# The uncast first w1 piece of an attention and soft-MoE kernel, loaded in three transfers of 32, 32 and 64 partitions instead of one of 128

## The chip, the cores and the metric

The kernel runs on one core of a Trainium2 chip. The metric is the device time of one execution in microseconds. Five executions of the kernel before took 178.75 to 179.28 us, with a median of 178.91 us.

## What is computed

The reference has two stages. The first is attention in 8 batches of 8 heads, 576 tokens and a head size of 64. Heads 0 to 3 see the last 32 tokens, heads 4 to 7 see every fourth of the last 128. The second stage takes the attention output as 4608 rows of 512 and sends it through a soft mixture of 8 experts with 4 slots each:

```python
scores = np.where(masks, scale * (q @ k.T), -1e9)          # per batch and head
x = (softmax(scores) @ v)                                   # -> 4608 x 512
logits = x @ phi                                            # 4608 x 32 slots
slot_input = softmax(logits, over tokens).T @ x             # 32 x 512
for e in range(8):
    h = np.maximum(slot_input[e] @ w1[e], 0.0)              # w1[e]: 512 x 1024
    slot_out[e] = h @ w2[e]                                 # w2[e]: 1024 x 512
out = softmax(logits, over slots) @ slot_out                # 4608 x 512, float32
```

All inputs and the output are float32. The two expert matrices come to 2 MB each per expert, q, k and v to 9.4 MB each, the output to 9.4 MB.

## The kernel before

The kernel is one program of scheduled operations. Each is declared with `op(engine, function, duration, priority, reads, writes)`. A planner (`Sched.run`) simulates the engines and one DMA queue with the estimated durations. It picks the order of the operations on each engine, and `emit` then writes them out with semaphore waits taken from the declared reads and writes.

**Loads.** q, k and v come in 16 half-batches (4 heads each, L334) of three transfers, and the weights in 35 further pieces (w1 by L344, w2 by L352 and L359). All of them are issued by GpSimd (POOL), because they are cast from float32 to bf16 on the way. Their order is fixed in `dma_order`: k, q, v of a half-batch, then one or no weight piece, and the rest of the weights after the last half-batch. The staging buffers of q, k and v hold four half-batches, so a later load waits until VectorE has transposed what stands in its buffer (L477, L483).

**The one load that is not cast.** The first half of expert 0's w1 (rows 0 to 255, 1 MB) is issued by SyncE (SP) at L387, as the first instruction of its queue. It lands as float32 in the space that w2 of expert 4 takes much later (`w2off(4)`). Partition p gets rows 2p and 2p+1, which are 8 KB in one run. ScalarE (ACT) then casts it to bf16 in two halves (L392, 1024 columns each) into w1's place. ACT's first other work is the exponential of the first scores (L537). SP's next instruction is the load of phi (L454), after that come only the output stores (L911).

**Compute.** Each half-batch goes through transposes on VectorE (L477), scores on TensorE (L498 to L522), the exponential on ACT (L537), the transpose of v (L559, L565), the product with v (L592 to L616), normalisation on VectorE (L599, L603), and, after each second half-batch, the logits and the slot sums (L682 to L736). When all are done, the experts run: L808 to L832 for w1, L847 for w2. The w2 products start as their pieces arrive. The output tiles (L890, evicted by L899 and L902) are stored by SP. Columns 0 to 255 of three row groups can go before the last w2 pieces are there.

The transfer in question and its readers:

```python
op(SP, lambda: spq.dma_start(af(w2off(4), [[1, 2048]]), moe_w1[0, 0:256, :].rearrange(...)),
   ..., sem=sem("s_w1f"), writes=b_w2[4], name="w1f")
for x in range(2):
    op(ACT, ..., reads=b_w2[4], writes=[b_w1[0]], name=f"w1c{x}")
```

Of the kernel before, what the change touches and what calls it, by code (L numbers as in the profile page):

```python
# [54 lines left out]
class Sched:  # L55
# [8 lines left out]
    def op(self, eng, fn, dur, prio, reads=(), writes=(), rmw=(), after=(), banks=(), name="",  # L64
           kind="c", nbytes=0, rate=422e3, lag=0.0, sem=None, tail=False):
        o = Op()
        o.eng, o.fn, o.dur, o.prio, o.name = eng, fn, dur, prio, name
        o.kind, o.bytes, o.rate, o.lag, o.sem, o.tail = kind, nbytes, rate, lag, sem, tail
        o.deps, o.succ = set(), []
        o.banks, o.opens, o.ord = [], [], None  # L70
        o.seq = len(self.ops)
        for a in after:
            if a is not None:
                o.deps.add(a)
        for b in reads:
            o.deps.update(b.w)
            b.r.append(o)
        for b in writes:
            if b.r:
                b.prev = b.w + b.r  # L80
                b.w, b.r = [], []
            o.deps.update(b.prev)
            b.w.append(o)
        for b in rmw:
            o.deps.update(b.prev)
            o.deps.update(b.w)
            o.deps.update(b.r)
            b.w.append(o)
        for b in list(reads) + list(writes) + list(rmw) + list(banks):
            if isinstance(b, Bank) and b not in o.banks:  # L90
                o.banks.append(b)
                if b.left == 0:
                    o.opens.append(b)
                b.left += 1
        o.deps.discard(o)
        self.ops.append(o)
        return o
# [99 lines left out]
def bass_dilated_sliding_attn__then__soft_moe_slots_kernel(  # L197
# [65 lines left out]
    def af(off, dims, p0=0, pn=128):  # L263
        return AP(ar_f.tensor, (p0 * NBF + off) // 2, [[NBF // 2, pn]] + dims)
# [12 lines left out]
    op = sc.op  # L277
    PE, ACT, DVE, POOL, SP = "PE", "ACT", "DVE", "POOL", "SP"
    pe, act, dve, pool, spq = nc.tensor, nc.scalar, nc.vector, nc.gpsimd, nc.sync
# [26 lines left out]
    b_w2 = [[Buf(f"w2{e}{s}") for s in range(2)] for e in range(8)]  # L306
# [6 lines left out]
    def w2off(e):  # L313
        return o_w2 + e * 8 * DM if e < 5 else o_stg + (e - 5) * 8 * DM


    def sem(n):
        return [nc.alloc_semaphore(n), 0]
# [54 lines left out]
    def load_w(n):  # L373
# [10 lines left out]
                   lag=(2.9 if name[2] == "s" else 2.3) if name[:2] == "w2" else 0.8, prio= -100.0 if nw[0] < 2 else -80.0, name=name, writes=list(wr) + rd)  # L384


    op(SP, lambda: spq.dma_start(  # L387
        af(w2off(4), [[1, 2048]]),
        moe_w1[0, 0:256, :].rearrange("(p two) f -> p (two f)", two=2)), .1, -200.0,
       kind="dma", nbytes=1 << 20, sem=sem("s_w1f"), writes=b_w2[4], name="w1f")  # L390
    for x in range(2):
        op(ACT, lambda x=x: act.activation(  # L392
            a(o_w1 + 1024 * x, [[1, 1024]]), af(w2off(4) + 2048 * x, [[1, 1024]]), ACTF.Copy),
# [379 lines left out]
    for x, y in zip(dma_order, dma_order[1:]):  # L773
# [7 lines left out]
       writes=[b_rcol], name="cs")  # L781
# [19 lines left out]
    for x in range(2):  # L801
# [12 lines left out]
        for g in range(2):  # L814
# [5 lines left out]
            writes=[b_hsb[x], b_p[0], b_p[1]], name=f"RL{x}")  # L820
# [39 lines left out]
    for y in range(2):  # L860
# [3 lines left out]
       name="SOx")  # L864
# [139 lines left out]
```

## Time and profile before

| | |
|---|---|
| five executions | 178.75 to 179.28 us, median 178.91 us |
| the profiled execution | 179.28 us, of which the span from first to last instruction is 177.5 us |
| busy share: TensorE, VectorE, ScalarE, GpSimd | 72%, 66%, 59%, 28% |
| mean granted TensorE clock | 0.938 |
| DMA | 41.29 MB written, mean 233 GB/s; HBM read and written 402 GB/s |
| queue of the GpSimd loads (q0) | 30.41 MB, 90.8% of 16 engines' span |
| queue of the SyncE transfers (q1) | 10.55 MB, 15.7% |
| the transfer of L387 | 1024 KB, issued at 0.74 us, landed after 5.0 us |

The profile counts DMA by what is written. A GpSimd load writes bf16 and reads twice as much, so 212 GB/s of such loads are 424 GB/s of reading. The DMA share is the time that packets took, divided by the time of 16 DMA engines. It can pass 1 because packets of one DMA engine overlap a little. The q0 and q1 queues are served by the same 16 DMA engines.

### The profile page before, as it was taken

Reading aid. Unit: us, or ns where it says so; the run is one execution under the profiler, and the core shown is the slowest. Engines: PE = TensorE matmul, PEld = TensorE weight load, DVE = VectorE, ACT = ScalarE, POOL = GpSimd, SP = SyncE. Lnnn points to the kernel's source line nnn. Section 1 sums busy time; section 2 is a strip of 40 time slices with the busy share of each in tenths; the row PEclk is TensorE's granted clock in tenths of the full one; section 3 lists DMA queues with packets and bytes.
Section 4 is the critical chain, followed back from the end, with each engine's and each line's share of the span. In section 5 each row is a group of like instructions: output and inputs, shape, how many; then the busy total and the mean of one; then the engine's idle time right before and its main releaser. Section 6 shows DMA issues by size and latency. Waiting matters only on the chain.

```text
span 177.5 us, 5201 instructions
## 1 busy us (share of the span) xinstructions
PE 127.8 (72%) x2173; PEld 86.6 (49%) x2174; DVE 117.7 (66%) x224; ACT 105.2 (59%) x166; POOL 50.3 (28%) x100
## 2 busy tenths in 40 slices
PE   0019768885999989889879988996596658698000
PEld 0006556664767677567567667684443223341000
DVE  6889578798899999798588999653300013499300
ACT  2406298886889799779748979794202012299000
POOL 7469931423413432332770000392000000000000
PEclk9999999999999999999978999999969987999655
DMA  5999999999999999999999999999999999999997
GB/s 188 229 211 215 214 207 212 216 206 212 217 210 208 217 207 211 217 209 210 215 207 212 213 210 217 213 212 214 213 215 210 203 196 178 285 321 398 417 423 314
DMA packets 19606, 41.29 MB, mean 233 GB/s; under 512 B 1920, under 2 KB 9088, under 8 KB 18688
## 3 DMA queue, kind: packets, MB, share of 16 engines
q0 software_dynamic: 15024, 30.41, 90.8%
q1 hardware_dynamic: 4560, 10.55, 15.7%
q8 instruction: 17, 0.28, 0.6%
q14 instruction: 5, 0.04, 0.1%
HBM read 61.93 MB, written 9.44 MB: 402 GB/s over the span
## 4 chain that ended last, share of the span: by engine, by line
DMA 34%; PE 33%; DVE 12%; ACT 7%; issue 3%; POOL 3%; POOLq 1%; DVEq 0%; ACTq 0%
DMA ar<-in_moe_w_dram 19%; DMA ar<-in_k_dram 15%; PE ps L498 8%; PE ps L559 4%; ACT ar L537 4%; PE ps L890 4%; DVE ar L477 3%; PE ps L592 3%; PE ps L505 3%; POOL ar L359 2%; PE ps L515 2%; PE ps L682 2%; DVE ar L433 2%; PE ps L649 2%; PE ps L725 1%
## 5 line engine op out<-in xcount | busy, mean ns | idle before, releaser
L477 DVE STREAM_TRANSPOSE ar<-ar 128x576 uint32<-128x576 uint32 x40 | 48.8, 1244 | 2.9 <-DMA ar<-in_k_dram 2.9
L537 ACT ACTIVATE ar<-ps 128x1152 bf16<-128x1152 f32 (+1 forms) x32 | 37.9, 1186 | 21.3 <-PE ps L505 8.8
L498 PE MATMUL ps<-ar 128*128 128x320 bf16 (+1 forms) x128 | 23.9, 312 | 14.3 <-DVE ar L477 12.9
L603 DVE TENSOR_TENSOR ar<-ps,fs 96x768 bf16<-96x768 f32 (+1 forms) x32 | 26.1, 818 | 1.1
L565 ACT ACTIVATE ar<-ps 128x768 bf16<-128x768 bf16 x32 | 24.8, 809 | 3.1 <-PE ps L559 2.8
L498 PEld LDWEIGHTS ps<-ar 128*128 128x128 bf16 x128 | 10.8, 101 | 19.7 <-POOL ar L406 12.8
L592 PE MATMUL ps<-ar 128*128 128x65 bf16 x320 | 15.5, 198 | 4.8 <-ACT ar L537 3.2
L559 PE MATMUL ps<-ar 128*128 128x128 bf16 x192 | 16.1, 229 | 3.0 <-DVE ar L603 2.2
L899 ACT ACTIVATE ar<-ps,fs 128x256 f32<-128x256 f32 (+1 forms) x24 | 11.5, 626 | 9.0 <-PE ps L890 9.0
L592 PEld LDWEIGHTS ps<-ar 128*128 128x128 bf16 x320 | 12.8, 101 | 7.4 <-issue 2.9
L847 PE MATMUL ps<-ar 128*32 128x512 bf16 (+1 forms) x80 | 12.0, 359 | 5.1 <-DMA ar<-in_moe_w_dram 4.0
L334 POOL DMA_DIRECT2D ar<-in_k_dram x16 | 9.0, 560 | 21.1 <-DVE ar L477 18.7
L559 PEld LDWEIGHTS ps<-ar 128*128 128x128 bf16 x192 | 12.6, 118 | 4.6 <-issue 1.9
L902 DVE TENSOR_SCALAR ar<-ps,fs 128x256 f32<-128x256 f32 (+1 forms) x24 | 12.8, 607 | 1.0 <-PE ps L890 1.0
L599 DVE RECIPROCAL fs<-ps 96x12 f32<-96x12 f32 (+1 forms) x32 | 6.4, 200 | 10.0 <-PE ps L592 9.5
L352 POOL DMA_DIRECT2D ar<-in_moe_w_dram x12 | 6.4, 580 | 22.0 <-DVE ar L477 22.0
L334 POOL DMA_DIRECT2D ar<-in_q_dram x16 | 8.8, 552 | 12.3 <-DVE fs L599 6.3
L334 POOL DMA_DIRECT2D ar<-in_v_dram x16 | 8.9, 555 | 10.8 <-DVE ar L477 5.2
L890 PE MATMUL ps<-ar 128*128 128x256 bf16 (+1 forms) x47 | 10.0, 329 | 1.7 <-DVE ar L871 1.0
L659 ACT ACTIVATE ar<-ps 128x576 bf16<-128x576 bf16 x16 | 9.5, 652 | 2.1 <-PE ps L643 1.9
L847 PEld LDWEIGHTS ps<-ar 128*32 128x32 bf16 x80 | 5.0, 100 | 11.7 <-DMA ar<-in_moe_w_dram 3.4
L682 PE MATMUL ps<-ar 128*128 128x288 bf16 x64 | 9.2, 287 | 1.2 <-ACT ar L666 1.2
(76 smaller groups left out, 187.5 us busy)
## 6 DMA issues: line engine op xcount, KB each, us to landing
ar<-in_moe_w_dram POOLq DMA_DIRECT2D x29, 512.0 KB, 26.2
out_dram<-ar SPq DMA_DIRECT2D x6, 1024.0 KB, 8.3
ar<-in_k_dram POOLq DMA_DIRECT2D x16, 288.0 KB, 22.2
ar<-in_q_dram POOLq DMA_DIRECT2D x16, 288.0 KB, 22.5
ar<-in_v_dram POOLq DMA_DIRECT2D x16, 288.0 KB, 22.8
out_dram<-ar SPq DMA_DIRECT2D x11, 256.0 KB, 3.3
ar<-in_moe_w_dram SPq DMA_DIRECT2D x1, 1024.0 KB, 5.0
ar<-in_moe_w_dram POOLq DMA_DIRECT2D x2, 256.0 KB, 31.6
```

Source lines behind the costliest of these rows:

```text
L334: return pool.dma_start(a(o_stg + (s * 3 + j) * 1152, [[1, 1152]]), src[b, 4 * dl:4 * dl + 4].rearrange("h (p t) d -> (h p) (t d)", p=32))
L477: return dve.transpose(au(o_dst, [[1, 18], [18, 32]]), au(src, [[32, 18], [1, 32]]))
L498: pe.matmul(pf(h, 0, [[1, W]]), a(o_id, [[1, 128]]), a(msk, [[1, W]]), start=True, stop=False)
L537: eo = op(ACT, lambda P=P, W=W: act.activation(a(P, [[W, 4], [1, W]]), AP(ps, 0, [[4096, 128], [512, 4], [1, W]]), ACTF.Exp, scale=SCALE), ...
L559: last = pe.transpose(pb(bank.idx, bb * 256 + par * 32, [[64, 4], [1, 32]]), src, a(o_id, [[1, 128]]))
L565: op(ACT, lambda t=t, bank=bank: act.activation(a(o_vb[vs] + 3 * t * VBK, [[66, 12], [2, 32], [1, 2]]), pb(bank.idx, 0, [[64, 12], [1, 32] ...
L592: last = pe.matmul(pf(bank.idx + x, 65 * t, [[1, 65]]), w, a(VB + t * VBK + 66 * h, [[1, 65]]), start=True, stop=True)
L603: op(DVE, lambda hp=hp, bank=bank: dve.tensor_tensor(a(ox + 128 * hp, [[64, 2], [256, NT], [1, 64]], 0, rows), pf(bank.idx, 0, [[512, 2], ...
L682: last = pe.matmul(pf(bank.idx, 0, [[1, 288]]), a(o_phis + 128 * c, [[1, 128]]), a(o_xt[xt] + 576 * c + 288 * g, [[1, 288]]), start=(c == ...
L847: last = pe.matmul(pf(sobank[x].idx, 0, [[1, n]], 32 * j, 32), a(o_htz + 1024 * g + 128 * c + 32 * j, [[1, 32]]), a(w2off(e) + DM * c + co ...
L890: op(PE, lambda: pe.matmul(pf(bank.idx, 0, [[1, cw]]), a(o_et + 512 * G + j, [[4, 128]]), a(o_so + c0, [[1, cw]]), start=True, stop=True), ...
L902: op(DVE, lambda: dve.tensor_scalar(dst, src(), sca, None, op0=AluOp.mult), dvet(cw, True) + .08, prio + .1, reads=[bank, b_rinv], writes= ...
```

## The change

The one transfer of L387 becomes three, over partitions 0 to 31, 32 to 63 and 64 to 127, issued by SP one after the other. Each has 8 KB per partition as before, and the bytes, their source and their place are the same. All three raise the same semaphore, so ACT's first cast waits until it stands at 48 instead of 16.

```diff
-    op(SP, lambda: spq.dma_start(
-        af(w2off(4), [[1, 2048]]),
-        moe_w1[0, 0:256, :].rearrange("(p two) f -> p (two f)", two=2)), .1, -200.0,
-       kind="dma", nbytes=1 << 20, sem=sem("s_w1f"), writes=b_w2[4], name="w1f")
+    s_w1f = sem("s_w1f")
+    for p0, pn in ((0, 32), (32, 32), (64, 64)):
+        op(SP, lambda p0=p0, pn=pn: spq.dma_start(
+            af(w2off(4), [[1, 2048]], p0, pn),
+            moe_w1[0, 2 * p0:2 * (p0 + pn), :].rearrange("(p two) f -> p (two f)", two=2)), .1, -200.0,
+           kind="dma", nbytes=pn << 13, sem=s_w1f, writes=b_w2[4], name=f"w1f{p0}")
```

The order of the instructions on TensorE, ScalarE, VectorE and GpSimd is the same in both programs; SP has two instructions more.

## The prediction

> **What bounds the kernel now.** I read the 40 slices first, then the queues, then the chain that ended last, and then went into the first microseconds, where the change lies. The slices and the queues:
>
> ```profile
> DMA  5999999999999999999999999999999999999997
> GB/s 188 229 211 215 214 207 212 216 206 212 217 210 208 217 207 211 217 209 210 215 207 212 213 210 217 213 212 214 213 215 210 203 196 178 285 321 398 417 423 314
> q0 software_dynamic: 15024, 30.41, 90.8%
> DMA 34%; PE 33%; DVE 12%; ACT 7%; issue 3%; POOL 3%; POOLq 1%; DVEq 0%; ACTq 0%
> ```
>
> The DMA engines are busy from the second slice to the last. No compute engine is: TensorE, the busiest, stands at 72%. The GpSimd loads move 206 to 217 GB/s in nearly every slice until about 145 us (twice that in reading), and the stores about 420 GB/s at the end. The chain names DMA for only 34%, but it has these long steps in it:
>
> ```profile
> 61.30 25.74 DMA ar<-in_k_dram
> ...
> 119.62 33.90 DMA ar<-in_moe_w_dram
> ```
>
> A 288 KB load needs 1.4 us of the engines at this rate and lands 22 to 26 us after its issue: it stands in a queue. Such a backlog makes the end of the load stream a plain sum: its start plus the work in it. After the last weights (153.5 us) come the last w2 products, the output tiles and the stores, which follow it at a fixed distance. So what the change does to the moment at which the 16 DMA engines get to the queued loads, it does to the end of the kernel, one for one. Windows over the stretch from 20 to 140 us show a share of 1.07 to 1.09 and 211 to 213 GB/s in each 20 us, so there is no idle stretch in which a delay could be made good.
>
> Now the start, first the instructions, then the DMA share in half microseconds (the last two columns are DMA share and GB/s):
>
> ```profile
> 0.74 0.38 SPq L387 DMA_DIRECT2D ar<-in_moe_w_dram  x1
> ...
> 1.24 0.68 POOL L334 DMA_DIRECT2D ar<-in_k_dram  x1 [0.80 <-POOLq L989]
> ...
> 5.74 2.00 ACT L392 ACTIVATE ar<-ar 128x1024 bf16<-128x1024 f32 x2 [3.72 <-DMA ar<-in_moe_w_dram]
> ...
> 14.62 1.13 ACT L537 ACTIVATE ar<-ps 128x1152 bf16<-128x1152 f32 x1 [6.88 <-PE ps L505]
> ```
>
> ```profile
> 1.50:2.00 0.50, 0.00 (x0) 0.00 (x0) 0.50 (x1) 0.50 (x1) 0.50 (x2) 1.00 0.76 131
> 2.00:2.50 0.50, 0.00 (x0) 0.00 (x0) 0.50 (x1) 0.02 (x1) 0.50 (x2) 1.00 0.39 66
> 2.50:3.00 0.50, 0.00 (x0) 0.00 (x0) 0.35 (x1) 0.00 (x0) 0.50 (x2) 1.00 0.74 246
> 3.00:3.50 0.50, 0.00 (x0) 0.00 (x0) 0.37 (x1) 0.00 (x0) 0.50 (x3) 1.00 1.06 442
> 3.50:4.00 0.50, 0.00 (x0) 0.00 (x0) 0.50 (x1) 0.00 (x0) 0.50 (x2) 1.00 0.98 410
> ...
> 5.00:5.50 0.50, 0.00 (x0) 0.00 (x0) 0.22 (x2) 0.00 (x0) 0.50 (x3) 1.00 1.04 232
> ```
>
> Two things are to be seen. The transfer is alone on the DMA engines until about 4.7 us, and only from 5 us does the rate fall to that of the cast loads. Between 1.75 us, where its first packets start, and 3 us there is a ramp with little moved. The records of the single packets in the trace say it finer. Eight packets start at 1.75 to 1.83 us, one for each of eight DMA engines, and the other eight engines start at 2.55 to 2.75 us. Four packets end by 2.14 us, then none before 2.85. From 3.0 us every engine moves 8 KB in 309 ns (26.5 GB/s). Four engines, which got two packets through early, finish their eight packets at 4.71 to 4.83 us, the other twelve at 5.12 to 5.36. Each engine's first packet of the GpSimd queue starts within about 10 ns of that, and no engine takes one before: w1f goes first, whole.
>
> **The change, part by part.** *Two more issues on SP.* At 0.38 us each (the row of L387) they end at about 1.9 us instead of 1.12. SP's next instruction is the load of phi at 11.65 us, which waits 10.5 us for VectorE: nothing.
>
> *Two more completions.* The completion packet took 9 ns on each engine. Two more are 0.02 us of the stream. I count it with the rest.
>
> *The cast.* ACT's first cast now waits for three transfers. Behind it on ACT stands the second cast and then L537, which starts at 14.62 us after 6.88 us of idling. Only if w1f landed more than 6.9 us later would that cover be gone; then each further microsecond would delay the first exponential by as much. The first q, k and v have cover too: the first k load's packets end by 6.8 us, VectorE takes it at 10.38 after its memsets. Two microseconds hurt nobody here.
>
> *No order changes.* Per engine the instructions stand as before, so no other instruction is moved past a queue.
>
> *The time of the pieces on the DMA engines.* This decides. Before, 8 packets of 309 ns make 2.47 us per engine. No transfer in this trace writes a part of the partitions, so the price is bounded. The low end is no change: 16 engines share each piece, two packets each in 32 partitions, 309 ns a packet. For the high end take what the trace shows of the destination. With 128 partitions over 16 engines, eight partitions take 26.5 GB/s, and in no row does a group of eight take more. If that is a limit of the partitions and not only of the engine, 32 partitions take 106 GB/s and 64 take 212. One by one, the pieces then need 2.47 us each, 7.4 in all: +4.9 us. Between the ends, the pieces are issued 0.38 us apart, so the first two are in flight together: 512 KB into 64 partitions, 2.47 us. The third has its packets behind theirs on every engine, and so follows: another 2.47. That gives 4.94 us, +2.47, and I take this one. It lies nearest to what the rows say: 26.5 GB/s for a group of eight, and engines that go through a queue in order.
>
> [...]
>
> *The ramp.* The change may take something out of the 1.25 us between 1.75 and 3.0 us. If the pause stays, each engine still has one packet done at 3.0 us and seven to go: 3.0 + 7 x 0.618 = 7.3 us, against 5.1 to 5.4 now, about +2.0 (the first packet is paid inside the pause). If smaller pieces remove the pause, 1.75 + 4.94 = 6.7 us, +1.4. I cannot tell them apart: the pause falls into the setup of the 128-partition transfer, but four engines that had begun at 1.79 us were stuck in it as well. I take +1.8.
>
> *Sum.* The profiled execution took 179.28 us, the span of 177.5 and 1.78 around it. The load stream ends 1.8 later, the stores follow: span 179.3, execution 181.1. That execution was the slowest of the five; on the median of 178.91 it makes **180.7 us**. A difference of about 0.2% (0.36 us) is what a measurement of this kernel can tell from no change.
>
> **The rivals.** *The ramp is the whole effect, faster.* If eight partitions can take more than 26.5 GB/s, the narrow pieces cost nothing, and the smaller first piece reaches all 16 engines at once instead of eight at 1.75 us and eight at 2.55. Ideal would be 1.75 + 8 x 0.309 = 4.2 us for all engines against 5.1 to 5.4 now: -0.9 to -1.1. With half of the pause left it is -0.5, 178.4 us. It decides as soon as a packet of the narrow pieces takes under about 0.42 us: then the loss (8 x 0.11 = 0.9 us) is smaller than the largest gain. For it speaks that the second eight engines start 0.8 us late; against it, that four early engines gained nothing from an early start.
>
> *Nothing to see.* The pause is a cost of the first reading of HBM and stays, and the packets stay at 309 ns: 178.9 us, give or take 0.3.
>
> *Interleaving softens it.* The GpSimd loads are issued from 1.24 us. In three pieces, w1f may let them in between, and while some engines do those, the others have the partitions for themselves. The work lost shrinks to +0.4 to +1.0, 179.6 us. w1f then lands later: phi, issued at 11.65 us, got its first packet at 15.13, so a piece may wait 3.5 us. Two such waits would put the landing at 12.7 us and use up ACT's cover of 6.9, so this would cost only a tenth or two on ACT. Against it: no engine let a GpSimd packet in before its w1f was done.
>
> **How the numbers follow.** Narrow pieces slow, +1.0 to +2.5 us: 0.58. Softened, +0.4 to +1.0: 0.09. Nothing to see: 0.11. Ramp, -0.4 to -1.1: 0.22. So faster 0.22, same 0.11, slower 0.67. The first case alone spans 179.9 to 181.4. The ramp case holds more than a tenth, so the range goes down into it, to 178.2; upward it ends at 181.4, which leaves out the end where all three pieces run singly (+4.9).
>
> **What would show it right or wrong.** In the changed profile, windows of half a microsecond between 3 and 7 us should show about 210 GB/s instead of 410 to 440, the rate of the cast loads should begin at about 7 us, and the casts of L392 at about 7.5 to 8 instead of 5.74, with L537 still near 14.6. The last weights should land 1.8 us later than 153.5 us, and everything behind them should keep its distance. If those windows show 400 GB/s or more before 3 us, and the casts start before 5.4, the ramp rival is right. If the casts start later and the end stays, then I have misjudged that the load stream carries its delay to the end.

## The result and the profile after

The changed kernel takes 180.90 us (median of 24 executions) against 179.27 us (45 executions of the kernel before). The ratio is 1.008 with a 95% interval of 1.0061 to 1.010: about 1.4 us slower, 1.1 to 1.8. Ratios leave out executions over 1.5% above the fastest of their kernel (three of the changed kernel's, 182.8 to 183.4 us), and the profile of run e6 below is of such an execution. The profiled execution took 180.15 us, its span is 178.3.

The same half microseconds at the start, in the profile after (the last two columns are the DMA share and GB/s):

```profile
1.50:2.00 0.50, 0.00 (x0) 0.00 (x0) 0.50 (x1) 0.50 (x1) 0.50 (x2) 1.00 0.85 197
2.00:2.50 0.50, 0.00 (x0) 0.00 (x0) 0.50 (x1) 0.02 (x1) 0.50 (x2) 1.00 0.75 229
2.50:3.00 0.50, 0.00 (x0) 0.00 (x0) 0.35 (x1) 0.00 (x0) 0.50 (x2) 1.00 1.29 328
3.00:3.50 0.50, 0.00 (x0) 0.00 (x0) 0.37 (x1) 0.00 (x0) 0.50 (x2) 1.00 0.72 147
3.50:4.00 0.50, 0.00 (x0) 0.00 (x0) 0.50 (x1) 0.00 (x0) 0.50 (x3) 1.00 1.04 175
```

A window counts a packet's whole time and bytes where the packet starts. So a single share can jump (1.29, then 0.72), and what a row tells is the GB/s for its share. Below I also use the packet records of the trace, with each packet's bytes spread evenly over the time that it took.

Until 3.0 us the change brings what one might hope for: spread in this way, 304 KB are moved by then, against 163 KB in the kernel before. From 3.0 us, where the windows of the kernel before show 442 and 410 GB/s at a share of 1.06 and 0.98, they show 147 and 175 at 0.72 and 1.04. Spread evenly, the share is 1.01 and 0.95, at 221 and 181 GB/s: the engines are busy and move about half. The sixteen packets that start from 3.10 to 3.76 us take 643 ns each on average, where 309 ns was the rule. The GpSimd loads come in at 3.74 us, between the second piece and the third, and the last data packet of w1f ends at 8.96 us instead of 5.36.

The instructions around it, and the landing times from the page:

```profile
0.73 1.44 SPq L390 DMA_DIRECT2D ar<-in_moe_w_dram  x3
...
9.89 2.00 ACT L395 ACTIVATE ar<-ar 128x1024 bf16<-128x1024 f32 x2 [7.87 <-DMA ar<-in_moe_w_dram]
...
14.62 1.13 ACT L540 ACTIVATE ar<-ps 128x1152 bf16<-128x1152 f32 x1 [2.73 <-PE ps L508]
```

```profile
ar<-in_moe_w_dram SPq DMA_DIRECT2D x2, 256.0 KB, 3.7
ar<-in_moe_w_dram SPq DMA_DIRECT2D x1, 512.0 KB, 8.2
```

The casts start 4.15 us later, and it costs nothing: L540 starts at 14.62 us as before, ACT only idles less ahead of it. The end of the kernel is decided elsewhere. In the chain that ended last, the long DMA steps are

```profile
36.18 25.35 DMA ar<-in_k_dram
...
76.44 26.00 DMA ar<-in_k_dram
...
122.77 32.04 DMA ar<-in_moe_w_dram
```

The last step ends at 154.8 us; before it ended at 153.5. So the load stream came later by that much, and the stores after it. In this pair of profiles the spans differ by only 0.8 us. Single executions differ by more than that, so I go by the ratio, and by the stream itself.

**A measure used below: the delay of the load stream.** Every GpSimd load ends on each of the 16 DMA engines with a completion packet (in the kernel before 1328 packets of 4 bytes for 83 loads, 22 ns each in the median). I take the 41st load, which completes at about 73 us in the kernel before, and average over the engines how much later it completes. In the changed kernel that is +1.27 us. It is +1.34 near 14 us and +1.28 at 149 us, so what was lost in the first ten microseconds stays as it is through the whole stream.

Where the delay comes from can be added up from the same records, as time per DMA engine (a sixteenth of the sum). The packets of w1f took 4.04 us instead of 2.92, which is +1.12. Eight GpSimd packets that ran among them took 713 to 1273 ns where 192 is the rule: +0.39. Completion packets of w1f: +0.08. Between 1.74 and 9 us an engine stood idle for 0.24 us instead of 0.48 (counted where fewer than sixteen packets ran): -0.24. That makes +1.35, beside the +1.34 measured near 14 us. The same sum comes within 0.2 us of the delay in every other run but e3 and e10, where it is too large because packet records overlap.

### The profile page after: what moved, and what is told of

It is laid out like the page before. It is cut to its first block, busy times and chain, and to the rows that moved or that the text cites. A ratio compares the mean times of both kernels' runs of the same rounds, so it can differ in the third digit from the quotient of the medians.

```text
span 178.3 us, 5203 instructions
## 1 busy us (share of the span) xinstructions
PE 128.2 (72%) x2173; PEld 86.2 (48%) x2174; DVE 117.9 (66%) x224; ACT 105.5 (59%) x166; POOL 50.4 (28%) x100
## 4 chain that ended last, share of the span: by engine, by line
DMA 56%; DVE 12%; PE 11%; POOL 7%; issue 4%; ACT 2%; POOLq 1%; DVEq 0%
DMA ar<-in_k_dram 38%; DMA ar<-in_moe_w_dram 18%; DVE ar L480 3%; PE ps L893 3%; POOL ar L359 3%; PE ps L562 2%; POOL ar L334 2%; DVE ar L905 2%; DVE ar L436 2%; PE ps L501 2%; DVE ar L606 1%; DVE ar L441 1%; PE ps L508 1%; ACT ar L902 1%; POOL ar L409 1%
## 5 line engine op out<-in xcount | busy, mean ns | idle before, releaser
L540 ACT ACTIVATE ar<-ps 128x1152 bf16<-128x1152 f32 (+1 forms) x32 | 37.9, 1186 | 17.2 <-PE ps L525 10.8
L501 PE MATMUL ps<-ar 128*128 128x320 bf16 (+1 forms) x128 | 23.3, 307 | 14.9 <-DVE ar L480 12.9
L501 PEld LDWEIGHTS ps<-ar 128*128 128x128 bf16 x128 | 10.6, 100 | 20.1 <-POOL ar L409 12.8
L595 PE MATMUL ps<-ar 128*128 128x65 bf16 x320 | 14.8, 195 | 4.7 <-ACT ar L540 3.2
L595 PEld LDWEIGHTS ps<-ar 128*128 128x128 bf16 x320 | 12.3, 98 | 7.3 <-issue 2.7
L334 POOL DMA_DIRECT2D ar<-in_k_dram x16 | 8.9, 559 | 22.6 <-DVE ar L480 14.8
L562 PEld LDWEIGHTS ps<-ar 128*128 128x128 bf16 x192 | 12.4, 118 | 5.4 <-PE ps L595 1.8
L334 POOL DMA_DIRECT2D ar<-in_v_dram x16 | 8.9, 554 | 13.3 <-DVE ar L480 7.0
L850 PE MATMUL ps<-ar 128*32 128x512 bf16 (+1 forms) x80 | 10.7, 337 | 2.2 <-DMA ar<-in_moe_w_dram 1.5
L334 POOL DMA_DIRECT2D ar<-in_q_dram x16 | 8.8, 551 | 10.8 <-DVE fs L602 4.9
L685 PE MATMUL ps<-ar 128*128 128x288 bf16 x64 | 10.1, 306 | 1.2 <-ACT ar L669 1.2
L665 ACT ACTIVATE ar<-ps 128x1024 bf16<-128x1024 bf16 x8 | 8.2, 1022 | 3.1 <-PE ps L652 3.1
```

What stands on the lines that cost most here:

```text
L334: return pool.dma_start(a(o_stg + (s * 3 + j) * 1152, [[1, 1152]]), src[b, 4 * dl:4 * dl + 4].rearrange("h (p t) d -> (h p) (t d)", p=32))
L501: pe.matmul(pf(h, 0, [[1, W]]), a(o_id, [[1, 128]]), a(msk, [[1, W]]), start=True, stop=False)
L540: eo = op(ACT, lambda P=P, W=W: act.activation(a(P, [[W, 4], [1, W]]), AP(ps, 0, [[4096, 128], [512, 4], [1, W]]), ACTF.Exp, scale=SCALE), ...
L562: last = pe.transpose(pb(bank.idx, bb * 256 + par * 32, [[64, 4], [1, 32]]), src, a(o_id, [[1, 128]]))
L595: last = pe.matmul(pf(bank.idx + x, 65 * t, [[1, 65]]), w, a(VB + t * VBK + 66 * h, [[1, 65]]), start=True, stop=True)
L850: last = pe.matmul(pf(sobank[x].idx, 0, [[1, n]], 32 * j, 32), a(o_htz + 1024 * g + 128 * c + 32 * j, [[1, 32]]), a(w2off(e) + DM * c + co ...
```

## The experiments

Three theories stood against each other. **W**: the pieces are too narrow, and the sixteen engines get in each other's way in the same partitions. **P**: each extra transfer costs by itself, through its setup or because it lets GpSimd loads in. **S** came up on the way: rows are handed to the engines at a limited pace, and small rows leave them idle. All edits are at the place of the change. The order of compute instructions is that of the kernel before, but for one small VectorE instruction in e4 and for e3, where the planner ordered the work of TensorE, VectorE and ScalarE differently from about 31 us on.

| run | pieces | delay of the stream, us | ratio to before (95%) |
|---|---|---|---|
| the change | 32, 32, 64 partitions | +1.27 | 1.008 (1.0061 to 1.010) |
| e11 | the same again | +1.12 | one execution |
| e1 | 128 partitions, 512, 512, 1024 columns | +0.98 | 1.0058 (1.0023 to 1.0092) |
| e2 | 64, 64 | +1.38 | 1.0062 (1.0024 to 1.010) |
| e3 | eight of 16 | +3.74 | one execution |
| e4 | one of 128, and 1 MB more | +2.40 | 1.016 (1.009 to 1.023) |
| e5 | 128 partitions, 1024, 1024 columns | +0.43 | 1.0019 (0.9983 to 1.0056) |
| e6 | every 4th, every 4th, every 2nd partition | +0.56 | 1.0031 (1.000 to 1.0063) |
| e7 | 64 from SP, 64 from ACT | +1.43 | 1.0094 (1.0062 to 1.0127) |
| e8 | 32 each, from 0, 64, 32, 96 | +0.96 | 1.009 (1.0055 to 1.0124) |
| e9 | 64 even, 64 odd partitions | +0.13 | 1.002 (0.9991 to 1.005) |
| e10 | 32 each, from 0, 32, 64, 96 | +1.63 | one execution |

The intervals of the ratios are some 0.3% wide to either side (0.7% in e4), so verdicts rest on the delay and the packet times, which come from one profile each. The one repeat (e11) differs from the first by 0.15 us. The three single executions took 185.33 (e3), 183.02 (e10) and 181.82 us (e11), more than their delays make; I draw nothing from these times.

**Does a delay at the start go to the end? (e4)**

```diff
+    op(SP, lambda: spq.dma_start(af(w2off(3), [[1, 2048]]),
+        moe_w1[0, 0:256, :].rearrange("(p two) f -> p (two f)", two=2)), .1, -200.0,
+       kind="dma", nbytes=1 << 20, sem=sem("s_w1g"), writes=b_w2[3], name="w1g")
```

> The one 128-partition transfer as before, and behind it a second transfer of the same 1 MB to a place that is not needed until later (w2 of expert 3). Extra DMA work of 2.47 us per engine at the start and nothing else. If a delay at the start of the load stream goes to the end one for one, the kernel takes 2.3 to 2.6 us more (ratio 1.013 to 1.015); if slack somewhere takes part of it up, less than 2 us (below 1.011).

The stream is 2.40 us late at 73 us, 2.43 near 14 us and 2.46 at 149 us, for 2.47 us of extra engine time. The ratio of 1.016 is 2.9 us, and 2.4 lies well inside its interval (1.6 to 4.1). So the stream passes a delay at its start on, one for one, and nothing takes it up.

**By columns instead of partitions (e1).**

```diff
-    for p0, pn in ((0, 32), (32, 32), (64, 64)):
+    for c0, cw in ((0, 512), (512, 512), (1024, 1024)):   # all 128 partitions, columns c0 to c0 + cw
```

> Three transfers of the same sizes as in the changed kernel (256, 256 and 512 KB), but each over all 128 partitions, cut by columns (512, 512 and 1024 of 2048). Theory W, the width of a piece costs: packets here run at the full rate of an engine again (about 77 ns for 2 KB and 155 ns for 4 KB), w1f is through by 5.4 us or earlier, and the load stream is not delayed; if the small first piece also takes the pause at the start away, the kernel is up to 0.5 us faster than before: ratio 0.997 to 1.001. Theory P, the number of pieces costs (two more requests, GpSimd loads let in between): the same delay of the load stream as in the changed kernel, +1.2 to +1.5 us, ratio 1.006 to 1.010.

Neither theory foresaw what came. The packets are quick, as W has it (about 84 ns for 2 KB in the first microsecond), but the stream is late by 0.98 us all the same. Two later windows of e1:

```profile
3.50:4.00 0.50, 0.00 (x0) 0.00 (x0) 0.50 (x1) 0.00 (x0) 0.50 (x2) 1.00 0.71 194
4.00:4.50 0.50, 0.00 (x0) 0.00 (x0) 0.50 (x2) 0.00 (x0) 0.50 (x2) 1.00 0.68 137
```

The kernel before has a share of 0.98 and 0.94 there. This time the engines are not only slower, they have nothing to do for part of the time: up to 9 us an engine stands idle for 0.99 us, against 0.48 in the kernel before. Nearly all of the difference lies between 3 and 6 us; up to 3 us the kernel before is almost as idle (0.49 against 0.57 us). The rest of the delay is in w1f's packets, 3.22 us per engine instead of 2.92. The cut by columns has three times as many rows (384 of 2 and 4 KB instead of 128 of 8 KB). That led to theory S, tried with half the cuts.

**Two cuts by columns (e5).** The list becomes `((0, 1024), (1024, 1024))`, 256 rows of 4 KB.

> Two transfers over all 128 partitions, 1024 columns each, so rows of 4 KB and 256 rows in all (three transfers by columns had 384 rows of 2 and 4 KB and left the DMA engines idle in between). Theory S, the engines wait for the rows of small transfers to be handed out, about 128 rows in 0.9 us: at 4 KB a row that is 580 GB/s, more than the engines take, so no idle time and a load stream delayed by 0 to 0.4 us, ratio 0.999 to 1.002. Theory P, each extra transfer costs by itself: +0.5 to +0.7 us, ratio 1.003 to 1.004.

The delay is +0.43 us, just above what S allowed and a little below P's band. It is less than half of e1's. An engine is idle for 0.46 us, no more than in the kernel before (0.48), which fits S; the packets of w1f take 3.22 us per engine instead of 2.92, which S does not speak of. S's 128 rows in 0.9 us were an estimate that no run measured, and I don't call S shown.

**Halves, and the same halves laid out differently (e2, e9).** This pair decides between W and P. Both are two transfers of 64 rows of 8 KB from SP. The partitions differ, and with them the rows of w1 that each transfer reads, since partition p always gets rows 2p and 2p+1.

```diff
-    for p0, pn in ((0, 32), (32, 32), (64, 64)):
+    for p0, pn in ((0, 64), (64, 64)):                    # e2
+    for p0, st, pn in ((0, 2, 64), (1, 2, 64)):           # e9: partitions p0, p0 + st, ...
```

> Two transfers of 64 partitions each. [...] Theory P: one extra request instead of two, about half of the changed kernel's cost, +0.6 to +0.8 us, ratio 1.003 to 1.005, with packets of 309 ns wherever no GpSimd packet runs beside them.

> Two transfers of 64 rows of 8 KB as in the two halves, but over the even and then the odd partitions. Nothing else differs from the two halves, which delayed the load stream by 1.4 us. Theory W, the place of the rows costs: packets near 309 to 322 ns once all engines run, and a delay between -0.4 and +0.4 us, ratio 0.998 to 1.002. Theory P, the cutting costs: +1.2 to +1.5 us again, ratio 1.007 to 1.008.

The windows of e2 from 3 to 4 us and from 5 to 7, then those of e9:

```profile
3.00:3.50 0.50, 0.00 (x0) 0.00 (x0) 0.36 (x1) 0.00 (x0) 0.50 (x3) 1.00 0.98 246
3.50:4.00 0.50, 0.00 (x0) 0.00 (x0) 0.50 (x1) 0.00 (x0) 0.50 (x2) 1.00 1.33 279
...
5.00:6.00 1.00, 0.00 (x0) 0.00 (x0) 0.56 (x3) 0.00 (x0) 1.00 (x5) 1.00 1.02 243
6.00:7.00 1.00, 0.00 (x0) 0.00 (x0) 1.00 (x1) 0.00 (x0) 0.57 (x4) 1.00 0.87 195
```

```profile
3.00:3.50 0.50, 0.00 (x0) 0.00 (x0) 0.36 (x1) 0.00 (x0) 0.50 (x3) 1.00 0.97 410
3.50:4.00 0.50, 0.00 (x0) 0.00 (x0) 0.50 (x1) 0.00 (x0) 0.50 (x2) 1.00 0.94 348
...
5.00:6.00 1.00, 0.00 (x0) 0.00 (x0) 0.57 (x3) 0.00 (x0) 1.00 (x5) 1.00 1.07 349
6.00:7.00 1.00, 0.00 (x0) 0.00 (x0) 1.00 (x1) 0.00 (x0) 0.58 (x4) 1.00 1.01 226
```

At the same share, e9 moves 410 GB/s where e2 moves 246. The packets of e2's second half take 514 to 551 ns (means of sixteen at a time), those of e9's second piece 322. The delay is +1.38 against +0.13 us, a difference of 1.25. It is all in the packets of w1f: they take 4.32 us per engine in e2 and 3.09 in e9, and the idle time is the same (0.46 and 0.47 us). The number of transfers, the size of their rows and their bytes are the same, so P is out as the main cause, and W is left in this form: packets take longer (514 to 551 ns against 322) when the engines work at the same time on rows that lie in the same part of the partitions.

One rival is not separated by any run: that the place of the rows in HBM counts, because each half of e2 reads one stretch of 512 KB. What speaks against it is that each load of q, k or v (L334) also reads one stretch, of 576 KB, and that these loads write to all 128 partitions and run at 424 GB/s of reading.

**The changed kernel's own three pieces, spread out (e6).** Partitions 0, 4, ..., then 2, 6, ..., then all odd ones.

```diff
+    for p0, st, pn in ((0, 4, 32), (2, 4, 32), (1, 2, 64)):
+        ... AP(ar_f.tensor, (p0 * NBF + w2off(4)) // 2, [[st * NBF // 2, pn], [1, 2048]]), ...[p0::st]
```

> Three transfers of 32, 32 and 64 rows of 8 KB as in the changed kernel, but the rows are every fourth partition (from 0, from 2) and every second (from 1), so that each piece reaches over the whole width. Theory W, the width of a piece sets the rate: packets of 309 ns instead of 615 to 650, no delay or a gain of up to 0.4 us, ratio 0.997 to 1.001. If what counts is which partitions the sixteen engines write at the same moment, two engines may still meet in the same group: packets near 600 ns and +1.0 to +1.4 us, ratio 1.005 to 1.008. Theory P: +1.2 to +1.4 us with packets of 309 ns.

The third piece's packets are back at 322 ns for the most part (371 in its first sixteen, 398 to 561 in the changed kernel). The first two pieces were mixed: 536, 342, 539 and 322 ns. The delay falls from 1.27 to 0.56 us, between the two outcomes that I had written down. The windows at 3.5 to 4.0 and 4.0 to 4.5 us have a share of 0.49 and 0.71, so part of what is left is idle time between the pieces (an engine is idle for 0.79 us, 0.31 more than in the kernel before).

**Narrower still (e3).** Eight pieces of 16 partitions.

> Eight transfers of 16 partitions. Theory W: a quarter of the width's rate, packets of about 1.2 us where all engines are in the same piece, and the load stream delayed by clearly more than in the changed kernel, +3 to +7 us. Theory P: seven extra requests instead of two, +4 to +5 us, but the packets stay near 309 ns where no GpSimd packet runs beside them. The packet times tell the two apart, not the total.

The stream is 3.74 us late; W foresaw 3 to 7 us, P 4 to 5. In order of their starts, sixteen at a time, the packets average 502, 428, 885, 344, 368, 984, 951 and 898 ns. Half of them are as slow as W has it (most took 0.8 to 1.07 us; the 1.2 foreseen was an estimate, about twice the 643 ns of the change). The fourth and fifth sixteen are quick although they overlap one another, which W does not explain. Completion packets are held up too: six near 4.7 us took 1.13 to 1.15 us.

**Order of the quarters (e8, e10).** `((0, 32), (64, 32), (32, 32), (96, 32))` and `((0, 32), (32, 32), (64, 32), (96, 32))`.

> Four transfers of 32 partitions in the order 0, 64, 32, 96. If the halves of the partitions are separate and two pieces in flight overlap, packets come down from 615 to 650 ns towards 309 and the delay of the load stream falls to +0.3 to +0.8 us, ratio 1.002 to 1.005. If the engines go through the pieces in step, each piece still has its half to itself: +1.2 to +1.6 us, ratio 1.007 to 1.009. Theory P: three extra transfers instead of two, +1.8 to +2.1 us, ratio 1.010 to 1.012.

> Four transfers of 32 partitions in the order 0, 32, 64, 96, to set beside the order 0, 64, 32, 96, which delayed the load stream by 1.0 us. If two pieces in flight get in each other's way only when they lie in the same half, this order is slower: +1.3 to +1.8 us of delay. If the order does not matter: +0.9 to +1.1.

In turn the delay is +1.63, alternating +0.96 us, with the same four transfers. So, as far as one profile each shows, neighbours in the same half hinder each other more than pieces in different halves. The alternating order came out better than "in step", and worse than full overlap; its ratio of 1.009 lies above what +0.96 us would make (1.005, just under the interval). Four pieces in alternation are also less late than the three of the change, which P cannot explain.

**Both halves at once (e7).** The upper half is issued by ACT, at the same 0.74 us as the lower by SP.

```diff
+    for p0, e, q_ in ((0, SP, spq), (64, ACT, act)):
+        op(e, lambda p0=p0, q_=q_: q_.dma_start(af(w2off(4), [[1, 2048]], p0, 64), ...
```

> Two transfers of 64 partitions, the lower half issued by SP, the upper by ScalarE at the same time, so that both halves of the partitions are written in the same microseconds. Theory W: each engine has packets for both halves, the sixteen need not meet in one half, and the whole lies between the full rate and half of it: load stream delayed by 0 to +0.7 us, ratio 0.998 to 1.004. Theory P: like the two halves on one queue, +1.1 us, ratio 1.006.

W's expectation for this run missed: the halves did not run side by side. The packets of SP's half run from 2.07 to 4.47 us, and those of ACT's half start at 3.85 and end at 6.86 us, most of them at 560 to 640 ns. The run is useful for another reason. The first GpSimd packet comes at 6.24 us, so here is the narrow transfer with no load in between: 2.07 to 6.86 us, and a delay of +1.43. The packets of w1f take 4.36 us per engine, 1.44 more than in the kernel before, and the idle time is the same (0.45 us): the whole delay is in the packets.

**Once more (e11).**

> The changed kernel itself once more, for a second profile on this chip. If its first profile is typical, the load stream is delayed by 1.2 to 1.5 us from 13 us on, the third piece's packets take 600 ns and more where several of them run together, and the casts begin between 9 and 10.5 us.

The delay is +1.12 us at 73 us and +1.30 near 14, the casts start at 9.89 us again, and the third piece's packets average 421 to 547 ns. The picture is the same, a little milder than expected (1.2 to 1.5 us and 600 ns and more).

No version beats the one transfer of 128 partitions. e9 comes nearest by its delay; its ratio and that of e5 cannot be told from 1.

## Why the prediction was right, point by point

**The bound, and that a delay at the start goes through to the end: right.** e4 shows it with +2.4 us of delay for 2.47 us of work, and every other delay holds from 14 to 149 us as well.

**That narrow pieces run at half the rate: right where it counts, too large as a mean.** Forecast were 618 ns for every packet. 643 were measured where all engines were in the second piece, 560 to 640 in most of e7's second half. But the 128 packets of the change average 505 ns and those of e7 545, because some are quick, at the start above all (21 of 128 in the change took 330 ns or less). So the 4.94 us of the sum came out as 4.04 in the change and 4.36 in e7. Some of what the packets of w1f were spared went to the eight GpSimd packets caught among them (0.39 us per engine), which the sum did not have.

The way I got to the half rate was wrong in one part. I had taken 26.5 GB/s for any eight partitions as the ceiling, by which 32 partitions alone take 106 GB/s. The first piece of the change brought its 256 KB in from 1.76 to about 3.15 us, that is 188 GB/s. The 64 partitions of e7's first half came in at 218 GB/s (512 KB from 2.07 to 4.47 us), near the 212 of that ceiling and not far above the 188; why, no run shows. What I had taken from the overlap of the first two pieces came out near by luck. Half of the rows can go at the rate of all 128: in e9, transfers of 64 rows on every second partition ran at 309 to 322 ns a packet after the first ones, where the one transfer of the kernel before took 309.

**The ramp: the term that made the difference.** I had two values, +2.0 if the pause stays and +1.4 if it goes, and put 1.8 between them. It goes: the changed kernel had moved 304 KB by 3.0 us against 163 KB before (packets spread over their time). At the 425 GB/s of the kernel before that is 0.33 us won. What the pause comes from, no run shows. The unmixed case, e7, needs 4.8 us from first to last packet, near the 4.94 of the sum, where the kernel before needs 3.6 with its pause. The lower value would have been the better forecast, and it is what the ratio shows (1.4). That it fits so well is partly luck, since the packets cost less than the sum had, and the GpSimd packets among them more.

**That w1f goes first, whole: wrong for three pieces.** GpSimd loads came in at 3.74 us, between the second and third piece, and the casts began at 9.89 us instead of the 7.5 to 8 that I had named. The rival of interleaving had this right, but not its price. e7, with no load in between, is late by 1.43 us, and the change, with loads in between, by 1.27. That is a tenth or two, not the 0.8 to 1.4 us that this rival took off, and e7 also began 0.3 us later. The sign named for 3 to 7 us, about 210 GB/s in each half microsecond, came out as a mean only: the eight windows run from 104 to 355, with 205 in the mean, w1f and loads together.

**The covers: right.** ACT still idled 2.73 us before its first exponential, and the two extra issues on SP ended at 2.17 us, long before phi at 11.65.

**The ramp rival, faster: half of its mechanism is there** (0.33 us won by 3 us), but its condition, packets under about 0.42 us, failed (505 ns in the mean). Its best case would be pieces that are spread and come early. e9 is spread, but its first packets start at 2.07 us instead of 1.75, and it moved 128 KB by 3 us, less than the 163 KB of the one transfer.

## What to carry to other kernels

When a queue of loads is backlogged from start to end, read a change at its start by the time at which the DMA engines are free for that queue, and carry it to the end one for one (in e4, 2.47 us of work at the start were 2.46 us at 149 us). Don't cut a transfer into blocks of adjacent partitions to get it started sooner: here the packets took up to twice as long (643 ns against 309), at the same busy share (0.98 at 246 GB/s in e2, 0.97 at 410 in e9). If it has to be cut, take every second partition with rows of 8 KB, as in e9 (+0.13 us), and look at GB/s beside the share.

## What the runs showed of the hardware that was not expected

- Three transfers with rows of 2, 2 and 4 KB (e1) left a DMA engine idle for 0.99 us between 1.74 and 9 us. It was 0.46 with two of 4 KB rows (e5), and 0.48 with the one transfer of 8 KB rows. Whether it is the rows that do it is not shown.
- A transfer of 64 partitions, or of rows 2 or 4 partitions apart, had its first packet at 2.06 to 2.07 us (e2, e6, e7, e9), those of 16, 32 or 128 adjacent partitions at 1.74 to 1.76, all issued at 0.73 or 0.74 us.
- A completion packet of 4 bytes, 9 ns in the kernel before, took up to 1.15 us in e3 and 1.08 in e10, close to data packets that were held up as well. In such a stretch the DMA share says little of the work done: one half microsecond of e3 shows 2.49 at 161 GB/s, and still 1.51 with the packets spread over their time.
